# Row statistics a step later, the second head's mask at a step's end, and weight pieces last in one step of a top-k attention and MLP kernel

## The chip, the cores and the metric

The kernel runs on one core of one Trainium2 chip. The metric is device time in microseconds (us). The kernel before takes 1806.68 us, the median of three runs that lie between 1806.41 and 1808.73. The profiled execution took 1802.7 us, and its span from first to last instruction is 1800.9 us; all times within the kernel below count from the start of that span. A difference of 0.2% (3.6 us) is about the smallest that can be told from no change.

## What is computed

The reference, cut to what matters (8 batches, 8 heads, 576 rows, head size 64, model width 512):

```python
scores = scale * np.matmul(q, k.transpose(0, 1, 3, 2))
kth = np.partition(scores, -32, axis=-1)[..., -32:-31]
scores = np.where(scores >= kth, scores, -1000000000.0)
attn = np.exp(scores - max); attn = attn / (attn.sum(-1) + 1e-9)
x = (attn @ v)                      # heads side by side: (8, 576, 512)
mu, var = mean(x), mean((x - mu) ** 2)
xn = (x - mu) / np.sqrt(var + 1e-06) * g_ln
out = x + np.maximum(xn @ w_ch1, 0.0) @ w_ch2    # 512 -> 2048 -> 512
```

q, k and v are float32. The two weight matrices arrive as float64 (a float32 array times a float64 scalar) and are turned into float32 inside the kernel. Everything on the matrix engine is float32.

## The kernel before

**Units and steps.** A unit is one tile of 128 query rows (or the last 64 rows, a "rest" unit) of one batch for a pair of heads, one "tile" t = 0, 1 per head. There are 160 units. The order of everything is written out by hand: the loop `for n in range(END)` emits one step after another, and each engine runs its own instructions in just the order in which they were emitted. Buffers and semaphores only make an engine wait; nothing is reordered by a scheduler.

**What a step holds.** Step n works on several units at once:

- `scores(n+1)` (L318 to L337): the score products of the next unit on PE into four short PSUM buffers, and four copies to SBUF on ACT.
- `select(n, 0..3)` (L354, L359): four rounds of "the eight largest" and "replace them" on DVE, which find the 32nd largest score. This is DVE's main work, about 9.6 us for a whole unit and about 5.3 to 5.6 us for a rest unit.
- `prepare(n-1)` (L371, L372): the exponent's bias from the largest and the 32nd largest score, two small operations on POOL.
- `mask(n-1, t)` (L375) on ACT, and `weigh(.., t)` (L384), the exponential on ACT with its row sum. For the first eight units (`EARLY`) mask and weigh follow each other in one step; later, weigh is in the step after the mask.
- `turn` (L408 to L438): transposes of the exponentials on PE (`tp`) and their copies to `pt` on ACT: part 0, part 1 and the last part.
- `values(g)` (L461, L468, L473) for a finished group of units: the product with v on PE (`av`), copied to `oT` on ACT.
- `place(g)` (L477, L500): transposes of `oT` on PE (`xo`), and the division by the sum on ACT, which writes the rows `x`. `place_rest` (L507) does this for the rows `r` of two batches' rest units.
- When a tile of rows has its last head pair, `arrived` calls `Block.stats` (L526 to L528): mean and variance on DVE and the subtraction of the mean ("centring") on POOL, in place. In the kernel before this is the last thing but a `fill` in the step that placed the rows, after `select(n, 3)`.

PSUM has five short buffers (`psps`), shared in turn by scores, `av`, `tp` and `xo`, and three for the MLP's sums.

**The MLP.** `Block.items` makes a list of MLP pieces for two or three tiles of rows: `turn` (L552, L557, the transposes of the rows), `hidden` (L565, first product, with a relu on ACT at L577 after each fourth) and `project` (L582, second product, finished on ACT at L591 and POOL at L595). `give(n)` puts a block on the list `todo` at a fixed step. `fill()`, called eight times in a step, takes pieces from the front of the list, in order, as long as an allowance `owed` lasts. The allowance grows by `share` per call, which is an eighth of the difference between the planned DVE time of the step and the planned PE time of its attention work. In some steps the planned PE time is the larger (steps that make a value product while a rest unit is in selection): the allowance grows by nothing there. What is left on the list at the end is emitted after the last step.

**Weight pieces.** 32 pieces of the weights are converted in steps -1 to 15, two at a time: `fetch`, then `split` (three ACT operations at L175 to L179 and a clamp on POOL at L180), a step later `shift` on DVE (L183) and `join` on POOL (L189, L193, L194). `weights(n, 0)` and `weights(n, 1)` stand before and in the middle of a step.

**The first rows' step.** Step 8 is special: the last unit of the first batch's first group (`quick`) is turned, multiplied with v and placed in one step, so that the first MLP block can start in step 9.

Of the kernel before, what the change touches and what calls it, by code (L numbers as in the profile page):

```python
# [9 lines left out]
AF = mybir.ActivationFunctionType  # L10
# [18 lines left out]
def kernel(  # L29
# [39 lines left out]
    nc = tc.nc  # L69
# [8 lines left out]
    scale = 1.0 / float(D) ** 0.5  # L78
# [131 lines left out]
    batches = {}  # L210
# [22 lines left out]
    todo = []  # L233
    share = [0.0]
    owed = [0.0]
# [7 lines left out]
        owed[0] -= cost  # L243
        run()

    def fill():
        owed[0] = min(owed[0] + share[0], 6.0)
        while todo and owed[0] >= todo[0][1] / 2 and (not todo[0][3] or todo[0][3]()):
            pop()


# [8 lines left out]
    def load(job, first, second):  # L260

        job.ins = {}
        for name, src, queue in (("k", k, first), ("q", q, second)):
            t = ldpool.tile([P, S], FP32, tag=name + "in", name=name + "in")
            for i in range(P // 32):
                head, d0 = 2 * job.hp + i * 32 // D, i * 32 % D
                queue.dma_start(
                    t[i * 32 : (i + 1) * 32, :].rearrange("b (n a) -> b n a", a=32),
                    src[job.b, head, :, d0 : d0 + 32].rearrange("(n b) a -> b n a", b=32),
                )  # L270
            job.ins[name] = t
# [93 lines left out]
    def prepare(u):  # L365

        nt = len(u.tiles)
        u.bias = small.tile([P, 2], FP32, tag="bias", name="bias")
        u.e = epool.tile([P, 2, S], FP32, tag="e", name="e")
        b = u.bias[:, 0:nt]  # L370
        nc.gpsimd.tensor_tensor(b, u.thr[:, 0:nt, 7], u.top[:, 0:nt, 0], ALU.subtract)  # L371
        nc.gpsimd.tensor_scalar_mul(b, b, scale)  # L372

    def mask(u, t):
        nc.scalar.activation(  # L375
            u.e[:, t], u.sc[:, t], AF.Prelu, bias=u.thr[:, t, 7:8], scale=-1.0, alpha=SLOPE
        )
# [64 lines left out]
    xs, xps, rs, oTr, dr = {}, {}, {}, {}, {}  # L442
# [69 lines left out]
    class Block:  # L512
        def __init__(self, tiles, dsts):
            self.n = len(tiles)
            self.tiles, self.dsts = tiles, dsts
            self.x = {}
            self.mv = None
            self.ready = False

        def stats(self, i):  # L520
            x = self.x[i]
            if self.mv is None:
                self.mv = small.tile([P, J, 2], FP32, tag="mv", name="mv")
                self.rstd = small.tile([P, J], FP32, tag="rstd", name="rstd")
            st = small.tile([P, 6], FP32, tag="st", name="st")
            nc.vector.bn_stats(out=st[:], in_=x)  # L526
            nc.vector.bn_aggr(out=self.mv[:, i, :], in_=st[:])
            nc.gpsimd.tensor_scalar_sub(x, x, self.mv[:, i, 0:1])  # L528

        def std(self):  # L530
            nc.scalar.activation(
# [8 lines left out]
        def items(self):  # L540
            n = self.n
            N = n * P
            xT = [None]
            hT = {}
            ps = {}

            def turn_x(i):
                if i == 0:
                    xT[0] = xtpool.tile([P, NC, 3 * P], FP32, tag="xT", name="xT")
                tp = turned()  # L550
                for c in range(NC):
                    nc.tensor.transpose(  # L552
                        tp[:, c * P : (c + 1) * P],
                        self.x[i][:, c * P : (c + 1) * P],
                        ident[:],
                    )
                nc.scalar.copy(  # L557
                    xT[0][:, :, i * P : (i + 1) * P],
                    tp[:].rearrange("p (c j) -> p c j", j=P),
                )  # L560

            def hidden(f, c):
                if c == 0:
                    ps["h"] = product("hps")
                nc.tensor.matmul(  # L565
                    ps["h"][:, 0:N],
                    w1[:, c, f * P : (f + 1) * P],
                    xT[0][:, c, 0:N],
                    start=(c == 0),
                    stop=(c == NC - 1),  # L570
                )
                if c == NC - 1:
                    per = J // n if n in (1, 2) else 1
                    if f % per == 0:
                        hT["h"] = hpool.tile([P, J * P], FP32, tag="h", name="h")
                    hT[f] = hT["h"][:, f % per * N : (f % per + 1) * N]
                    nc.scalar.activation(hT[f], ps["h"][:, 0:N], AF.Relu)  # L577

            def project(i, f):
                if f == 0:  # L580
                    ps["o"] = product("ops")
                nc.tensor.matmul(  # L582
                    ps["o"][:],
                    hT[f][:, i * P : (i + 1) * P],
                    w2[:, f, :],
                    start=(f == 0),
                    stop=(f == NF - 1),
                )
                if f == NF - 1:
                    o = opool.tile([P, DM], FP32, tag="o", name="o")  # L590
                    nc.scalar.activation(  # L591
                        o[:], ps["o"][:], AF.Identity,
                        bias=self.mv[:, i, 0:1], scale=self.rstd[:, i : i + 1],
                    )
                    nc.gpsimd.tensor_tensor(o[:], o[:], self.x[i], ALU.add)  # L595
                    for dst, rows in self.dsts[i]:
                        nc.sync.dma_start(dst, o[rows, :])

            per_row = 1.71e-3
            return (  # L600
                [("turn", 0.44, lambda i=i: turn_x(i), None) for i in range(n)],
                [
                    (
                        "hidden",
                        max(per_row * N, 0.31),
                        lambda f=f, c=c: hidden(f, c),
                        lambda f=f, c=c: done(ready[f * P // DM * NC + c]),
                    )
                    for f in range(NF)
                    for c in range(NC)  # L610
                ],
                [
                    (
                        "project",
                        per_row * DM,
                        lambda i=i, f=f: project(i, f),
                        lambda f=f: done(ready[NF + f]) and (f < NF - 1 or self.ready),
                    )
                    for i in range(n)
                    for f in range(NF)  # L620
                ],
            )
# [13 lines left out]
    units = []  # L636
# [11 lines left out]
    for j in jobs:  # L648
        j.twin = next((x for x in fresh if (x.b, x.hp) == (j.b, j.hp)), None)
        if j.twin is None:  # L650
            fresh.append(j)


    EARLY = jobs[NHP].first


# [77 lines left out]

        return max(0.0, dve_cost(n) - pe_cost(n)) / SLOTS

    recips = {}

    def arrived(key, x):
        blk, i = block_of[key]  # L740
        blk.x[i] = x
        blk.stats(i)

    load(fresh[0], nc.sync, nc.scalar)

    nc.scalar.copy(gcol[:, 0:1], eps[:])
# [9 lines left out]
    for n in range(END):  # L756
# [9 lines left out]
        parts = turn(ex) if ex else []  # L766
        early = ex is not None and n - 1 < EARLY
        last = ex and ex is ex.group.units[-1]

        if ex and not early:  # L770
            weigh(ex, 0)
# [5 lines left out]
            select(u, 0)  # L777
        for den in recips.pop(n, []):
            nc.vector.reciprocal(den, den)
        if mk:  # L780
            prepare(mk)
        if early:
            for t in range(2):
                mask(ex, t)
                weigh(ex, t)
        weights(n, 0)
        fill()
        if ex and len(ex.tiles) > 1 and not early:
            weigh(ex, 1)
# [7 lines left out]
        if n in turns:  # L797
            turn_heads(turns[n])
            later = fresh.index(turns[n]) + 1
            if later < len(fresh):  # L800
                load(fresh[later], nc.sync, nc.sync)
        for blk in gives.get(n - 1, []):
            blk.std()
        weights(n, 1)
        fill()
        if mk and not early:
            mask(mk, 0)
# [1 line left out]
            place(g)  # L809
        if late:  # L810
            place_rest(late.job.b, late.job.hp)
        fill()
        if mk and len(mk.tiles) > 1 and not early:
            mask(mk, 1)
        fill()
        if len(parts) > 2:
            parts[1]()
# [11 lines left out]
        fill()  # L829
        if parts:  # L830
            parts[-1]()
        fill()
        for x in (u if n < EARLY else None, mk if n > EARLY else None):
            if x and x is units[x.job.last]:
                load_values(x.job)
        quick = ex.group if last and ex.group.quick else None
        if quick:

            values(quick)
            for den in recips.pop(n + 1):  # L840
                nc.vector.reciprocal(den, den)
            place(quick)
        if u:
            select(u, 3)
        for x in (g, quick):
            if x and x.job.hp == NHP - 1:
                for qt in x.qts:
                    if qt < J:
                        arrived((x.job.b, qt), xs[x.job.b, qt])
        if late and late.job.hp == NHP - 1:  # L850
            r = late.job.b // 2
            arrived(("r", r), rs[r])
        fill()
    while todo:
        pop()
# [31 lines left out]
```

## Time and profile before

| what | value |
|---|---|
| time, median of 3 | 1806.68 us |
| span of the profiled run | 1800.9 us |
| PE matmuls | 1682.3 us busy, 7401 records |
| PE weight loads | 1011.0 us busy |
| DVE | 1500.0 us busy |
| ACT | 1145.3 us busy |
| POOL | 292.0 us busy |
| `max8` and `match_replace` (L354, L359) | 1451.7 us on DVE, about 745 ns each |
| `project` matmuls (L582) | 1152 records, 546.0 us |
| `hidden` matmuls (L565) | 2048 records, 551.5 us |
| all DMA | 66.69 MB, 37 GB/s over the span |

How to read it: a float32 matmul leaves two records in the trace, so 1152 records are 576 matmuls. Busy shares are averages over stages that differ much: up to 135 us there is no MLP work and PE waits; from there to 1621 us selection on DVE and MLP on PE run side by side; from 1621 us to the end there is only MLP work. A matmul's end is modelled in the trace, so the distance from one start to the next tells more of PE than its busy time does. Where a wait is for several semaphores, the one that came last is named.

### The profile page before, as it was taken

To read this page: it belongs to the slowest core of one execution; us is meant where nothing else is said; L and a number is where in the kernel's file an instruction comes from. 1 tells how busy PE (TensorE), PEld (TensorE's weight loads), DVE (VectorE), ACT (ScalarE), POOL (GpSimd) and SP (SyncE) were. 2 spreads that over 40 slices of the span, in tenths; PEclk is the share of its full clock that TensorE was granted. 3 is DMA by queue.
4 is the path that set the end of the run, shared out by engine and by line. 5 is a ranking of instruction groups with operands and counts; after the bars stand their busy time and mean duration, and the time that the engine had idled before them with its cause. 6 is when DMAs were issued, how large, how long until landed. Compare 5 with 4: busy or idle time off the path is not lost.

```text
span 1800.9 us, 23419 instructions
## 1 busy us (share of the span) xinstructions
PE 1682.3 (93%) x7401; PEld 1011.0 (56%) x7401; DVE 1500.0 (83%) x3144; ACT 1145.3 (64%) x2846; POOL 292.0 (16%) x545
## 2 busy tenths in 40 slices
PE   3669989999799999999999999999999999999998
PEld 2337456564454574655546665565545746575565
DVE  7869899999888999989998999899998999870000
ACT  6768876675565776667757776687667766682111
POOL 4665510100100111010111010111001010101000
PEclk9659999999899999999999999999999999999999
DMA  7423231002110112002110121101201210000000
GB/s 176 108 78 90 55 66 35 25 7 46 26 28 20 33 27 48 18 20 46 31 34 20 26 46 27 31 16 43 42 13 25 41 33 20 20 20 12 0 18 12
DMA packets 249348, 66.69 MB, mean 37 GB/s; under 512 B 240517, under 2 KB 240521, under 8 KB 249225
## 3 DMA queue, kind: packets, MB, share of 16 engines
q1 hardware_dynamic: 244488, 64.61, 16.1%
q10 hardware_dynamic: 4736, 0.59, 0.3%
q8 instruction: 59, 0.97, 0.2%
q14 instruction: 65, 0.52, 0.1%
HBM read 55.71 MB, written 9.44 MB: 36 GB/s over the span
## 4 chain that ended last, share of the span: by engine, by line
PE 54%; DVE 20%; issue 11%; ACT 9%; POOL 5%; DMA 0%; POOLq 0%; DVEq 0%; SPq 0%; ACTq 0%
PE ops L582 19%; PE hps L565 17%; DVE m L354 10%; DVE wk L359 8%; PE scps L337 7%; PE av L461 5%; PE tp L408 4%; ACT e L375 2%; ACT pt L420 2%; PE av L468 2%; ACT e L384 1%; ACT x L477 1%; POOL w L194 1%; POOL size L189 1%; POOL size L193 1%
## 5 line engine op out<-in xcount | busy, mean ns | idle before, releaser
L354 DVE MAX8 m<-wk 128x8 f32<-128x576 f32 x864 | 612.8, 746 | 2.0
L565 PE MATMUL hps<-xT,w 128*128 128x256 f32 (+1 forms) x2048 | 551.5, 414 | 2.0 <-ACT xT L557 1.4
L582 PE MATMUL ops<-w,h 128*128 128x512 f32 x1152 | 546.0, 604 | 0.0
L565 PEld LDWEIGHTS hps<-xT,w 128*128 128x128 f32 x2048 | 377.0, 193 | 111.2 <-issue 22.6
L359 DVE MATCH_REPLACE8 wk<-m,wk 128x576 f32<-128x576 f32 x576 | 423.7, 742 | 0.0
L582 PEld LDWEIGHTS ops<-w,h 128*128 128x128 f32 x1152 | 203.9, 193 | 185.9 <-issue 182.2
L337 PE MATMUL scps<-kT,qT 64*128 64x288 f32 (+3 forms) x1344 | 265.2, 442 | 45.2 <-ACT pt L420 17.3
L318 ACT COPY sc<-scps 128x288 f32<-128x288 f32 x576 | 198.7, 416 | 89.7 <-PE scps L337 82.1
L337 PEld LDWEIGHTS scps<-kT,qT 64*128 64x128 f32 (+1 forms) x1344 | 138.2, 181 | 179.2 <-issue 46.4
L384 ACT ACTIVATE e<-e,bias 128x576 f32<-128x576 f32 x288 | 227.8, 791 | 14.5 <-POOL bias L372 13.3
L354 DVE MAX8 m<-sc 128x8 f32<-128x576 f32 x288 | 203.3, 743 | 40.2 <-ACT sc L318 39.8
L408 PE MATMUL tp<-ident,e 128*128 128x128 f32 x1152 | 184.1, 285 | 49.4 <-ACT e L384 49.2
L408 PEld LDWEIGHTS tp<-ident,e 128*128 128x128 f32 x1152 | 145.8, 146 | 143.6 <-ACT e L384 69.5
L375 ACT ACTIVATE e<-sc,m 128x576 f32<-128x576 f32 x288 | 220.4, 779 | 0.9 <-DVE m L354 0.9
L359 DVE MATCH_REPLACE8 wk<-m,sc 128x576 f32<-128x576 f32 x288 | 211.9, 742 | 0.0
L420 ACT COPY pt<-tp 128x512 f32<-128x512 f32 x256 | 150.3, 587 | 78.5 <-PE tp L408 77.0
L577 ACT ACTIVATE h<-hps 128x256 f32<-128x256 f32 (+1 forms) x256 | 105.8, 413 | 145.4 <-PE hps L565 144.1
L461 PE MATMUL av<-pt,vb 128*64 128x256 f32 (+2 forms) x1088 | 148.7, 415 | 3.9 <-ACT pt L420 2.3
L371 POOL TENSOR_TENSOR bias<-m,m 128x2 f32<-128x2 f32 (+1 forms) x160 | 31.1, 194 | 688.1 <-DVE m L354 639.2
L461 PEld LDWEIGHTS av<-pt,vb 128*64 128x64 f32 x1088 | 73.6, 143 | 71.7 <-issue 24.8
L473 ACT COPY oT<-av 128x256 f32<-128x256 f32 (+2 forms) x68 | 26.2, 386 | 112.8 <-PE av L468 112.7
L595 POOL TENSOR_TENSOR o<-o,x 128x512 f32<-128x512 f32 x32 | 40.7, 1271 | 350.3 <-ACT o L591 345.4
(65 smaller groups left out, 1017.8 us busy)
## 6 DMA issues: line engine op xcount, KB each, us to landing
vb<-in_v_dram SPq DMA_DIRECT2D x136, 128.0 KB, 2.5
raw<-in_moe_w_ch_dram SPq DMA_DIRECT2D x32, 512.0 KB, 4.3
kin<-in_k_dram SPq DMA_DIRECT2D x128, 72.0 KB, 2.5
qin<-in_q_dram SPq DMA_DIRECT2D x120, 72.0 KB, 2.6
out_dram<-o SPq DMA_DIRECT2D x32, 256.0 KB, 2.1
ends<-in_v_dram SPq DMA_DIRECT2D x136, 16.0 KB, 2.2
dr<-den SPq DMA_DIRECT2D x64, 0.2 KB, 1.8
out_dram<-o SPq DMA_DIRECT2D x8, 128.0 KB, 2.4
```

The lines of the kernel that those rows point to most:

```text
L318: nc.scalar.copy(u.sc[:, t, s * HALF : (s + 1) * HALF], made[s][t][:, 0:HALF])
L337: nc.tensor.matmul(ps[i * R : i * R + ql, o : o + width], qT[r, q0 : q0 + ql], kT[r, k0 : k0 + width], start=True, stop=True,)
L354: nc.vector.max(m[:, t, :], u.cur[t])
L359: nc.vector.match_replace(u.wk[t][:], m[:, t, :], u.cur[t], LOWEST)
L375: nc.scalar.activation(u.e[:, t], u.sc[:, t], AF.Prelu, bias=u.thr[:, t, 7:8], scale=-1.0, alpha=SLOPE)
L384: nc.scalar.activation(u.e[:, t], u.e[:, t], AF.Exp, bias=u.bias[:, t : t + 1], scale=-scale / SLOPE, accum_out=g.den[:, col : col + 1],)
L408: nc.tensor.transpose(ps[:, c * P : (c + 1) * P], u.e[:, t, c * P + t * R : (c + 1) * P + t * R], ident[:],)
L420: nc.scalar.copy(g.pt[:, t * J : (t + 1) * J, q0 : q0 + P], ps[:].rearrange("p (c n) -> p c n", n=P),)
L461: nc.tensor.matmul(av[h * D : (h + 1) * D, 0 : g.nq], vb[:, h * J + c, :], g.pt[:, h * J + c, 0 : g.nq], start=(c == 0), stop=False,)
L565: nc.tensor.matmul(ps["h"][:, 0:N], w1[:, c, f * P : (f + 1) * P], xT[0][:, c, 0:N], start=(c == 0), stop=(c == NC - 1),)
L577: nc.scalar.activation(hT[f], ps["h"][:, 0:N], AF.Relu)
L582: nc.tensor.matmul(ps["o"][:], hT[f][:, i * P : (i + 1) * P], w2[:, f, :], start=(f == 0), stop=(f == NF - 1),)
```

## The change

The change has five parts.

1. `prepare` of the first 16 units (`CONVERTING` is 14 + 2) goes from POOL to ACT: a multiplication by the scale and one small activation per tile, three ACT operations instead of two on POOL. In these steps POOL is also converting weights.
2. Rows' statistics and centring wait for the following step: `arrived` only notes the rows for step n+1, and `blk.stats` runs there after `select(n, 1)`; for the very first rows (step 9, `gives_first`), already after `select(n, 0)`. A row tile's `turn` piece may be taken from the list only once its centring has been emitted (`centred`).
3. The mask of the second tile, `mask(mk, 1)`, goes from the middle of a step, ahead of the turns of parts 1 and last, to behind them.
4. The `fill` after `place` takes at least one piece, whatever the allowance, in steps that place rows.
5. In the first rows' step (`quick`, step 8), both halves of the weight pieces' work come after the rows have been placed.

The purpose is to take waits for ACT off DVE's queue, to take waits for POOL off ACT's, and to let copies out of PSUM come sooner.

```diff
-    def fill():
+    def fill(least=0):
         owed[0] = min(owed[0] + share[0], 6.0)
-        while todo and owed[0] >= todo[0][1] / 2 and (not todo[0][3] or todo[0][3]()):
+        while todo and (not todo[0][3] or todo[0][3]()):
+            if owed[0] < todo[0][1] / 2 and least <= 0:
+                break
+            least -= 1
             pop()
...
         b = u.bias[:, 0:nt]
+        if u.i < CONVERTING:
+
+            nc.scalar.mul(b, u.thr[:, 0:nt, 7], scale)
+            for t in range(nt):
+                nc.scalar.activation(
+                    b[:, t : t + 1], u.top[:, t, 0:1], AF.Identity,
+                    bias=b[:, t : t + 1], scale=-scale,
+                )
+            return
         nc.gpsimd.tensor_tensor(b, u.thr[:, 0:nt, 7], u.top[:, 0:nt, 0], ALU.subtract)
...
             nc.gpsimd.tensor_scalar_sub(x, x, self.mv[:, i, 0:1])
+            self.centred.add(i)
...
-                [("turn", 0.44, lambda i=i: turn_x(i), None) for i in range(n)],
+                [("turn", 0.44, lambda i=i: turn_x(i), lambda i=i: i in self.centred) for i in range(n)],
...
-    def arrived(key, x):
+    def arrived(n, key, x):
         blk, i = block_of[key]
         blk.x[i] = x
-        blk.stats(i)
-
+        rows_of.setdefault(n + 1, []).append((blk, i))
...
+        if n == gives_first:
+            for blk, i in rows_of.pop(n):
+                blk.stats(i)
...
-        weights(n, 0)
+        if not quick:
+            weights(n, 0)
         fill()
...
+        for blk, i in rows_of.pop(n, []):
+            blk.stats(i)
         for blk in gives.get(n - 1, []):
             blk.std()
-        weights(n, 1)
+        if not quick:
+            weights(n, 1)
...
-        fill()
-        if mk and len(mk.tiles) > 1 and not early:
-            mask(mk, 1)
+        fill(1 if g or late else 0)
         fill()
...
         if parts:
             parts[-1]()
+        if mk and len(mk.tiles) > 1 and not early:
+            mask(mk, 1)
         fill()
...
             place(quick)
+            weights(n, 0)
+            weights(n, 1)
```

More of the change, by code (lines that the diff above doesn't have):

```diff
@@ L517, in __init__ @@
             self.mv = None
+            self.centred = set()
             self.ready = False
@@ L651 @@
             fresh.append(j)
+    for i, u in enumerate(units):
+        u.i = i
+    CONVERTING = max(n for n in batches if batches[n]) + 2
     EARLY = jobs[NHP].first
@@ L735, in slot @@
         return max(0.0, dve_cost(n) - pe_cost(n)) / SLOTS
-    recips = {}
-    def arrived(key, x):
+    recips, rows_of = {}, {}
+    def arrived(n, key, x):
         blk, i = block_of[key]
         blk.x[i] = x
-        blk.stats(i)
+        rows_of.setdefault(n + 1, []).append((blk, i))
+    gives_first = min(gives)
     load(fresh[0], nc.sync, nc.scalar)
@@ L768 @@
         last = ex and ex is ex.group.units[-1]
+        quick = ex.group if last and ex.group.quick else None
         if ex and not early:
@@ L835 @@
                 load_values(x.job)
-        quick = ex.group if last and ex.group.quick else None
         if quick:
@@ L848 @@
                     if qt < J:
-                        arrived((x.job.b, qt), xs[x.job.b, qt])
+                        arrived(n, (x.job.b, qt), xs[x.job.b, qt])
         if late and late.job.hp == NHP - 1:
             r = late.job.b // 2
-            arrived(("r", r), rs[r])
+            arrived(n, ("r", r), rs[r])
         fill()
```

## The prediction

> **What bounds the kernel now.** I read the page first (busy shares and slices), then waits by engine, then sums by window, then the timeline of two stretches.
>
> ```profile
> PE 1682.3 (93%) x7401; PEld 1011.0 (56%) x7401; DVE 1500.0 (83%) x3144; ACT 1145.3 (64%) x2846; POOL 292.0 (16%) x545
> ...
> DVE  7869899999888999989998999899998999870000
> ```
>
> DVE stops in slice 36 of 40; about 180 us of pure MLP follow, the same 26 projects, two transposed blocks and their products in both builds, so the tail costs the same. Before there is any MLP work, from 45 to 90 and from 90 to 135 us, the windows view gives a granted PE clock of 0.65 and 0.56.
>
> DVE's waits, columns total, times, longest:
>
> ```profile
> DVE st L526 <- ACT x L477: 54.3, 13, 8.8
> DVE m L354 <- ACT sc L318: 39.8, 16, 4.8
> DVE size L183 <- POOL size L180: 12.4, 8, 2.9
> DVE den L779 <- ACT den L396: 9.6, 1, 9.6
> ...
> ACT e L384 <- POOL bias L372: 13.3, 5, 4.1
> ```
>
> The change takes the first row away almost whole. Whether that is time depends on the second: where DVE also waits for scores (m L354 <- sc), PE and ACT are the late ones, and a DVE that comes earlier only waits there longer. So look at PE in one period of 20 steps (windows view; PE, weight load, DVE, ACT, POOL busy):
>
> ```profile
> 768.00:962.00 194.00, 190.43 (x812) 102.39 (x812) 186.05 (x391) 132.42 (x326) 21.81 (x53) 0.99 0.15 31
> ```
>
> PE leaves 3.6 of 194 us, DVE 8. By distances from start to start (429 ns per 128x512 record when packed, 215 per 128x256, 322 per 128x384, 109 per transpose) PE is packed in nearly every step. The exceptions return: steps that place rows while a rest unit is selected, where the allowance gives no MLP piece (timeline, first PE, then ACT: start, length, engine, line, operation, out<-in, and in brackets the idle time before it and what ended it).
>
> ```profile
> 858.84 0.44 PE L500 MATMUL xo<-ident,oT 128*128 128x128 f32 x2
> 859.60 0.66 PE L408 MATMUL tp<-ident,e 128*128 128x128 f32 x4 [0.33 <-ACT e L384]
> 860.10 0.27 PE L437 MATMUL tp<-ident,e 128*128 128x128 f32 x1
> 860.30 2.02 PE L337 MATMUL scps<-kT,qT 64*128 64x288 f32 x6
> 862.70 0.75 PE L337 MATMUL scps<-kT,qT 64*128 64x288 f32 x2 [0.39 <-ACT pt L420]
> 863.38 1.25 PE L565 MATMUL hps<-xT,w 128*128 128x384 f32 x2
> ```
>
> ```profile
> 861.38 0.80 ACT L375 ACTIVATE e<-sc,m 128x576 f32<-128x576 f32 x1
> 862.04 0.61 ACT L420 COPY pt<-tp 128x512 f32<-128x512 f32 x1
> ```
>
> PE stands 0.49 us between xo and tp (859.11 to 859.60), and its scores take 3.1 us (860.30 to 863.38) where an unhindered set takes 1.17 (854.63 to 855.80): the fourth of the five short buffers comes free only with the copy at 862.04, which stands on ACT behind the second mask at 861.38. That is 2.4 us per such step, and there are 28 (30, 33, 36, 39, 42, 45, 48, 51, then four in each period).
>
> The start is another matter: POOL, ACT and PE hold one another up.
>
> ```profile
> 91.53 0.20 POOL L371 TENSOR_TENSOR bias<-m,m 128x2 f32<-128x2 f32 x1
> 91.60 0.43 DVE L183 TENSOR_SCALAR size<-size 128x512 uint32<-128x512 uint32 x1 [2.85 <-POOL size L180]
> ...
> 131.71 0.69 DVE L526 BATCH_NORM_STATS2 st<-x 128x6 f32<-128x512 f32 x1 [8.79 <-ACT x L477]
> ...
> 134.41 0.66 PE L552 MATMUL tp<-ident,x 128*128 128x128 f32 x4 [1.93 <-POOL x L528]
> ```
>
> **What the Trainium skill says.** "Perfetto Trace Analysis", Identifying the Most-Contended Engine: a PE's busy share is no measure of how full it is. The trace agrees: 93% busy, yet 4 of 20 steps hide 2.4 us. "TensorE: Matmul & The Clock Gate", Architectural detail (the array is 16x): ACT, DVE and GpSimd queues are strictly first in, first out. It agrees: the bias at 91.53 needed a result that DVE had at 82.0, and stood behind two weight pieces. Same page, What's actually happening: the clock is halved until activity lifts it; the 0.56 to 0.65 at the start agrees. Price: "ScalarE: Activation LUTs", What ACT_TABLE_LOAD costs: 186 ns plus 0.833 ns per element, about 93 ns more with a pointer bias, 93 ns overlapped.
>
> **Part by part.**
>
> Bias on ACT (16 units). The trace has no such operation; nearest is ACT den L396, 128x4 at 205 ns. By the page 0.19 + 2 x 0.28 - 2 x 0.09 = 0.56 us (estimate); if each waits for the one before, 0.9. I take 0.6. Against it stand the 13.3 us of waits for POOL's bias in the first eight units. Net by den of step 8 (before: 121.2): 13.3 - 8 x 0.6 = 8.5; about 1 goes where unit 1 is held by DVE instead; 7.6 us earlier. In steps 9 to 16 the bias only costs ACT; 1 us for that.
>
> Weight pieces last in step 8. Between den and the last copy to pt ACT loses six split operations at 0.57, of which 2.75 us reach the value product (its first record at 123.62, the bulk at 125.75, against pt copies that now follow each other). So x is ready 7.6 + 2.75 = 10.4 us earlier, near 121.6. But POOL now has split and join ahead of the centring: ACT size 0.7, clamp 0.6, joins 2 x (1.28 + 1.27) = 5.1, second clamp 0.6 bring it to 128.6; centring 1.6; first row transpose at 130.3 against 134.4. Gain 4.1 us. DVE reaches step 9 some 15 us earlier, but PE does not need it.
>
> Statistics in the next step. DVE's own 0.86 us per tile only move. Behind them stand selection rounds, which are then waited for by masks a step later; DVE is not late there. The 54.3 us of DVE waits are therefore worth nothing by themselves, save 1.2 at step 18 (the stage to 266 us is held by DVE: PE waits 3.39 us for qT at 265.66). A price comes where PE takes the rows at once. Step 31: PE is ready near 346; DVE starts the step at 344.1 (345.8 less two moved statistics), the statistics now come after select 1, 5.5 us into it, at 349.6, and the tiles are centred at 352.1 and 353.6. PE is back at the same piece 2.5 us later than before, step 30's gain already used up. Step 44: the r rows were taken at 471.91 after a wait of 6.39. Now 470.03 - 3.06 - 0.86 (wait and r statistics gone) + 5.62 + 0.86 + 1.67 = 474.26, less a tp part put ahead, 0.6: 1.75 us lost. Step 19 waits too, inside PE's spare time. All later blocks sit behind other pieces by steps: nothing.
>
> Mask at the end and a forced piece. The pt copy starts where the mask did, at 861.38 instead of 862.04: 0.66 us. The forced piece fills the gap and the wait for buffers, so its length (0.86, 0.64 or 0.43 us) vanishes from the packed step that follows; the instruction order of the build shows it taken from there. Step 42 has nothing to take; step 30 is used above. Of the other 26: 13 projects, 6 of 384, 7 of 256 columns: 11.2 + 3.8 + 3.0 = 18.0, plus 26 x 0.66 = 17.2: 35.2 us. The mask in its new place lies in ACT's waits for PE (0.8 us before the last copy and the relu). Step 16's forced piece: 1 us.
>
> End: the tp wait of 1.90 at 1619.6 shrinks, 1.5.
>
> Sum: 4.1 - 1 + 1.2 + 1 - 2.5 - 1.75 + 35.2 + 1.5 = 37.75. 1806.7 - 37.7 = 1769.
>
> Does DVE have room? Without waits it needs 186.6 us in the period 768 to 962; PE then needs 193.7 - (0.64 + 3 x 0.86 + 4 x 0.66) = 187.8. Just.
>
> **Rivals.**
>
> A: PE stays as packed as it is, and the new gaps fill only with waits (DVE or ACT comes last in those steps). Only the start and the turns count: 4.1 + 1.2 - 4.25, about 1, to 8 with half the terms: 1799 to 1806. For it: DVE's room of 1 us per period. Against: the waits named are ACT's, and DVE loses 5 us of waits per period.
>
> B: DVE is the bound and its waits come out whole: 54.3 + 12.4 = 67, 1740. For it: DVE at 83% and 94% in the middle. Against: PE's packing.
>
> C: slower. Centring lies behind the joins without x coming earlier (the ACT and PE round at the start not loosened): +4; steps 31 and 44 lose 5 and 4; no piece hidden: 1806.7 + 13 = 1820. For it: PE is in order, and a turn it cannot make stops everything. Against: only four blocks are taken at once.
>
> **How the numbers follow.** Forecast 0.74, A 0.12, B 0.09, C 0.05. Around the forecast: 0.66 and the piece's length could each be half true (17 us less gain), the start is worth 0 to 8, and better filled steps could spare PE clock dips (up to 8 more). That gives 1750 to 1788 with some of B's way; I give 1750 to 1790. Faster by over 0.2% needs under 1803: forecast, B and a half of A.
>
> **What would show it.** DVE st waits near zero, waits for sc larger than 39.8. First row transpose near 130. In the placing steps pt copies right after the x copies, and the last score pair 0.66 us sooner. PE waits for POOL's x near 6 us at step 31. If PE waits for e or DVE grow in the middle, A is right; if the start moves by much more than 4 us, my POOL queue is wrong.

## The result, and the profile after

| | before | after |
|---|---|---|
| median | 1806.55 us (4 runs, 1806.13 to 1808.73) | 1762.1 us (4 runs, 1760.61 to 1763.47) |
| ratio, 95% interval | | 0.9751, 0.9735 to 0.9768 |
| span of the profiled run | 1800.9 us | 1758.8 us |

The changed kernel is 44.5 us faster (2.5%); 1769 was forecast, with a range of 1750 to 1790. The profiled runs differ by 42.1 us. The forecast holds, but the sum behind it has a term missing and several that are too good, and the part of the change that its title names first, the later statistics, turns out to cost time.

The page of the changed kernel, the engines' busy time and the slices of DVE:

```profile
PE 1650.1 (94%) x7401; PEld 1003.4 (57%) x7401; DVE 1499.0 (85%) x3144; ACT 1153.3 (66%) x2894; POOL 285.6 (16%) x513
...
DVE  7988899989989999999999999999999999950000
```

DVE does the same work (1499.0 against 1500.0 us) in a shorter time. PE is busy 32 us less with the same 7401 records: the ends of matmuls are modelled, and time at half clock counts as busy.

DVE's waits of the changed kernel (total, times, longest):

```profile
DVE m L357 <- ACT sc L321: 35.5, 15, 8.2
...
DVE st L539 <- ACT x L489: 9.0, 2, 7.2
```

The wait for placed rows (`st`) is nearly gone, 54.3 to 9.0 us, but the wait for scores (`m <- sc`) did not grow in its place: 39.8 to 35.5. The sum of the two fell by 49.6 us, about as much as the kernel got shorter. Why that is no proof that DVE's waits were the cost is shown by the third experiment.

The period that the prediction looked at (20 steps; windows view: us, then PE, weight load, DVE, ACT and POOL busy, granted PE clock, DMA share, GB/s) now lies here in the changed kernel:

```profile
748.10:935.20 187.10, 186.72 (x820) 102.84 (x819) 185.56 (x390) 132.68 (x329) 21.76 (x53) 1.00 0.16 32
```

PE leaves 0.4 us of 187.1 (3.6 of 194 before), DVE 1.5 (8 before). The prediction put PE's need at 187.8 us and DVE's at 186.6, and said that DVE just has room. That is what came.

The placing step shown before at 858.84 now reads so on PE (timeline: start, length, engine, line, operation, out<-in, count):

```profile
841.74 0.44 PE L512 MATMUL xo<-ident,oT 128*128 128x128 f32 x2
842.01 0.81 PE L579 MATMUL hps<-xT,w 128*128 128x384 f32 x2
842.66 0.60 PE L420 MATMUL tp<-ident,e 128*128 128x128 f32 x4
843.10 0.27 PE L449 MATMUL tp<-ident,e 128*128 128x128 f32 x1
843.30 2.77 PE L340 MATMUL scps<-kT,qT 64*128 64x288 f32 x8
```

and so on ACT:

```profile
844.28 0.52 ACT L591 ACTIVATE h<-hps 128x384 f32<-128x384 f32 x1
844.65 0.62 ACT L432 COPY pt<-tp 128x512 f32<-128x512 f32 x1
845.11 0.32 ACT L450 COPY pt<-tp 128x128 f32<-128x128 f32 x1
845.27 0.84 ACT L387 ACTIVATE e<-sc,m 128x576 f32<-128x576 f32 x1
```

Between `xo` and `tp` stands the forced piece (842.01), where PE had been idle for 0.49 us, and the copy to `pt` (844.65) no longer has a mask ahead of it; the mask comes at 845.27, behind both copies. From start to start, the score products now take 2.70 us (843.30 to 846.00), which is 1.53 us more than a packed set; before it was 1.91 us. Of the 2.4 us that this step lost, 1.53 are left. It is one of the worst of its kind, since the relu of the piece (844.28) stands ahead of the copy to `pt`; in 9 of the 22 such steps after 474 us the scores lose 0.93 us only, in 9 more 1.15 to 1.25.

Two places that got worse. The turn of the rows placed in step 30, and that of the `r` rows, on PE (in brackets the idle time before and what ended it):

```profile
347.92 1.12 PE L566 MATMUL tp<-ident,x 128*128 128x128 f32 x4 [5.42 <-POOL x L541]
...
472.06 1.12 PE L566 MATMUL tp<-ident,r 128*128 128x128 f32 x4 [8.59 <-POOL r L541]
```

In the kernel before they read:

```profile
346.88 1.11 PE L552 MATMUL tp<-ident,x 128*128 128x128 f32 x4 [0.51 <-POOL x L528]
...
471.91 1.11 PE L552 MATMUL tp<-ident,r 128*128 128x128 f32 x4 [6.39 <-POOL r L528]
```

On DVE of the changed kernel, the statistics of the first stand behind two rounds of step 31's selection:

```profile
339.68 1.40 DVE L357 MAX8 m<-sc 128x8 f32<-128x576 f32 x2
...
345.22 0.69 DVE L539 BATCH_NORM_STATS2 st<-x 128x6 f32<-128x512 f32 x1
```

### The profile page after: what moved, and what is told of

The parts are those of the page before. It is cut to its first block, busy times and chain, and to the rows that moved or that the text cites. A ratio compares the mean times of both kernels' runs of the same rounds, so it can differ in the third digit from the quotient of the medians.

```text
span 1758.8 us, 23377 instructions
## 1 busy us (share of the span) xinstructions
PE 1650.1 (94%) x7401; PEld 1003.4 (57%) x7401; DVE 1499.0 (85%) x3144; ACT 1153.3 (66%) x2894; POOL 285.6 (16%) x513
## 4 chain that ended last, share of the span: by engine, by line
PE 63%; issue 10%; DVE 8%; ACT 4%; POOL 1%; POOLq 0%; DVEq 0%; ACTq 0%
PE hps L579 21%; PE ops L596 19%; PE scps L340 9%; PE av L473 6%; PE tp L420 5%; DVE m L357 4%; DVE wk L362 3%; PE av L480 2%; ACT e L387 1%; PE tp L566 1%; PE xo L512 1%; ACT oT L485 1%; PE tp L449 1%; ACT pt L432 1%; ACT x L489 0%
## 5 line engine op out<-in xcount | busy, mean ns | idle before, releaser
L340 PE MATMUL scps<-kT,qT 64*128 64x288 f32 (+3 forms) x1344 | 252.2, 441 | 33.5 <-DVE qT L296 20.1
L357 DVE MAX8 m<-sc 128x8 f32<-128x576 f32 x288 | 203.7, 744 | 36.3 <-ACT sc L321 35.5
L387 ACT ACTIVATE e<-sc,m 128x576 f32<-128x576 f32 x288 | 225.7, 784 | 1.5 <-DVE m L357 0.8
L473 PE MATMUL av<-pt,vb 128*64 128x256 f32 (+2 forms) x1088 | 144.7, 409 | 0.5 <-ACT pt L443 0.5
```

The source lines that it names most:

```text
L340: nc.tensor.matmul(ps[i * R : i * R + ql, o : o + width], qT[r, q0 : q0 + ql], kT[r, k0 : k0 + width], start=True, stop=True,)
L357: nc.vector.max(m[:, t, :], u.cur[t])
L387: nc.scalar.activation(u.e[:, t], u.sc[:, t], AF.Prelu, bias=u.thr[:, t, 7:8], scale=-1.0, alpha=SLOPE)
L473: nc.tensor.matmul(av[h * D : (h + 1) * D, 0 : g.nq], vb[:, h * J + c, :], g.pt[:, h * J + c, 0 : g.nq], start=(c == 0), stop=False,)
```

## Where the time went

I compared the start of every unit's score products on PE in the two traces (those of unit n + 1 stand in step n). The changed kernel is ahead of the kernel before by:

| up to | lead, us | what lies between |
|---|---|---|
| unit 31 | 4.1 | the start and step 16's piece |
| unit 34 | -0.4 | step 30's piece, and the turn of its rows, which waits: -4.5 |
| unit 45 | 4.4 | placing steps: +4.8 |
| unit 46 | 2.2 | turn of the `r` rows: -2.2 |
| unit 159 | 43.8 | 23 placing steps, and the clock: +41.6 |
| end | 42.1 | -1.7 |

The clock is the missing term. In the trace's record of the granted PE clock, the kernel before has six stretches at half clock between 474 and 1700 us, 27.3 us in all; the changed kernel has none. At half clock, half of that time is lost: 13.7 us. The steps bear this out: in five of them whose forced piece is a project piece the lead grows by 1.82 or 1.83 us up to the next score products, and in two more, where the kernel before had a stretch of 3.4 us behind the same place, by 3.52 and 3.53. What remains of the 41.6 us is 27.9. One placing step, near 490 us, is longer than the others in every kernel and has 0.3 of it; 22 like ones have about 1.25 us each.

One of these stretches, in the windows view of the kernel before, just behind the placing step of 858.84:

```profile
863.80:867.20 3.40, 3.40 (x7) 1.77 (x6) 3.40 (x8) 1.94 (x7) 2.48 (x4) 0.50 0.00 0
```

and the same place in the changed kernel:

```profile
846.70:850.10 3.40, 3.40 (x15) 2.11 (x14) 3.33 (x8) 3.37 (x12) 1.66 (x2) 1.00 0.43 68
```

In the first PE calls itself busy for all of the 3.40 us, at a clock of 0.50, with 7 records; in the second it does 15.

Stretches before 474 us are not counted here. Most of them lie at the start and at the two turns, where PE waits long. One matters below: at the turn of step 30's rows the kernel before has 6.8 us at half clock and the changed kernel 10.2.

## The experiments

The times of one table; "half clock" is the number and the total length of the stretches that begin between 474 and 1700 us in the profiled run.

| kernel | median, us | ratio to before, 95% interval | half clock |
|---|---|---|---|
| before (profiled run) | 1806.55 | | 6, 27.3 us |
| after | 1762.1 | 0.9751 (0.9735 to 0.9768) | 0 |
| e1 after, statistics at once | 1754.79 | 0.9709 (0.9688 to 0.973) | 1, 3.4 us |
| e2 before + piece + mask | 1754.64 | 0.971 (0.9692 to 0.9727) | 1, 3.4 us |
| e3 before + statistics later | 1821.73 | 1.0074 (1.0045 to 1.0102) | 12, 58.0 us |
| e4 after without the piece | 1781.62 | 0.986 (0.9842 to 0.9879) | 1, 6.8 us |
| e5 after without the mask's move | 1793.74 | 0.9921 (0.9904 to 0.9938) | 7, 30.7 us |
| e6 after, bias on POOL | 1766.48 | 0.9776 (0.9761 to 0.979) | 2, 6.8 us |
| e7 after, pieces as before | 1759.35 | 0.9733 (0.9718 to 0.9747) | 0 |
| e8 e1, centring ahead of the pieces | 1750.99 | 0.9689 (0.9674 to 0.9703) | 1, 6.8 us |
| e9 before + mask | 1771.37 | 0.9795 (0.9781 to 0.981) | 1, 3.4 us |
| e10 before + piece | 1787.21 | 0.9875 (0.9859 to 0.9892) | 7, 27.3 us |
| e11 before + start | 1812.56 | 1.0017 (1.0005 to 1.0029) | 7, 34.1 us |

The kernel before ran again beside each group: 1808.77 us beside e1 to e4, 1806.28 beside e5 to e8, 1807.68 beside e9 to e11. e5 to e8 ran on another chip than the rest of e1 to e11.

### Which part brings the gain: e1 to e4

The theory P is that of the prediction: PE is the bound, and its holes in the placing steps are the cost. D is the rival that DVE's waits for placed rows were the cost.

e1 puts the statistics back to the end of the placing step:

```diff
 def arrived(n, key, x):
     blk, i = block_of[key]
     blk.x[i] = x
-    rows_of.setdefault(n + 1, []).append((blk, i))
+    blk.stats(i)
```

> The kernel after, with only the statistics and the centring put back to the end of the step that placed the rows (the gate on the turn is then always open). Theory P (PE and its buffers are the bound, DVE comes second by about 1 us in a period of 20 steps): DVE gets its wait of some 5 us per period back, needs about 192 us in a period where the eased PE needs 187, so 4 to 5 us per period come back over five to six periods; the delays at steps 31 and 44 (4.9 and about 2 us in the trace of after) vanish. Together 1775 to 1790. Theory D (DVE's waits for the placed rows were the cost all along): nearly the whole gain is lost, 1798 to 1808.

Measured: 1754.79 us. Both theories missed, and the changed kernel gets faster without its moved statistics: the intervals of the ratios do not touch, and 0.9709 against 0.9751 is 7.6 us (5.6 between the profiled spans). DVE's waits of e1:

```profile
DVE st L539 <- ACT x L489: 26.8, 13, 8.4
DVE m L357 <- ACT sc L321: 20.1, 6, 5.6
```

My expectation for P was wrong in one point. I counted some 5 us in each period for a wait of DVE that comes back. It does come back, 26.8 us of it, but it is no cost of a fixed size: DVE stands ahead of PE and waits just as long as it is ahead, and a shorter wait for scores makes up for it (20.1 instead of 35.5). e1 is ahead of the changed kernel from one place on: at unit 32's score products its lead over the kernel before is 0.1 us, at unit 33's it is 3.7, where the changed kernel falls from 3.8 to -0.4. The same turn on PE in e1:

```profile
345.72 0.66 PE L566 MATMUL tp<-ident,x 128*128 128x128 f32 x4 [1.04 <-POOL x L541]
```

It waits 1.04 us instead of 5.42. So 4.4 of the 7.7 us that the two kernels differ by here are the wait. The clock has about 3 more, by estimate: the half-clock stretch of the changed kernel lasts from 343.9 to 354.1 us, 6.2 us beyond the end of the wait at 347.92, and e1 has none here. From unit 46 on the two kernels keep a distance of 3.4 to 6.3 us.

e2 goes the other way, the kernel before with only the forced piece and the mask's move (`fill(1 if g or late else 0)` and `mask(mk, 1)` behind the last turn, as in the change's diff):

> The kernel before, with only the forced piece after placing and the second mask at the step's end. P: the placing steps are eased (about 33 us, and some 10 us of PE clock dips), but DVE's waits remain and hold it back by 4 to 5 us a period: 1780 to 1793. D: the waits for placed rows stay, so at most 3 us: 1803 to 1807.

Measured: 1754.64 us, the same as e1. The two edits bring the whole gain and 7 us more; all else in the change costs that. The expectation of P was 25 us and more too slow, by the same mistake as in e1: without DVE's 4 to 5 us a period it had 43 us of gain, and 48.4 lie between the profiled spans.

e3 moves the statistics alone, with the condition on the `turn` piece:

```diff
-        blk.stats(i)
+        rows_of.setdefault(n + 1, []).append((blk, i))
...
+        for blk, i in rows_of.pop(n, []):
+            blk.stats(i)
         for blk in gives.get(n - 1, []):
             blk.std()
```

> The kernel before, with only the statistics in the following step (with the gate on the turn). P: PE is as packed as before, DVE only waits for scores in place of rows, and PE waits longer for centred rows at steps 31 and 44: 1805 to 1814. D: 1760 to 1770.

Measured: 1821.73 us, slower than both expected. D, by which DVE's waits were the cost, falls. DVE's waits of e3:

```profile
DVE m L354 <- ACT sc L318: 84.9, 38, 8.1
...
DVE st L527 <- ACT x L477: 15.3, 4, 8.8
```

The wait for rows went from 54.3 to 15.3 us and the wait for scores from 39.8 to 84.9: together 94.1 before and 100.2 now. The edit changes the name of DVE's wait, not its amount, because PE decides when DVE may go on. The trace also tells where the 21.3 us between the profiled spans went (1800.9 to 1822.2). The turn of step 30's rows waits 5.18 us on PE, and the lead is -5.1 us at unit 33's score products. The other loss is the clock: 58.0 us at half clock instead of 27.3, so 15.4 us more lost. That moved statistics bring such stretches is not shown: e11 below has 34.1 us without them, and e9 and e10 show how much of it is chance.

e4 is the changed kernel with `fill()` where the change has `fill(1 if g or late else 0)`:

> The kernel after, without the forced piece (the fill after placing keeps to its allowance). P: each of some 26 placing steps loses the length of its piece, 18 us in all, and a few PE clock dips come back: 1778 to 1788. D: the statistics are still moved, so 1762 to 1766.

Measured: 1781.62 us, as P has it. The forced piece is worth 19.5 us in the changed kernel, of which up to 3.4 are the one half-clock stretch of this kernel; 18.0 were predicted.

### The mask, and the clock: e5, e9, e10

e5 is the changed kernel with the second mask in the middle of the step:

```diff
         fill(1 if g or late else 0)
+        if mk and len(mk.tiles) > 1 and not early:
+            mask(mk, 1)
         fill()
...
         if parts:
             parts[-1]()
-        if mk and len(mk.tiles) > 1 and not early:
-            mask(mk, 1)
```

> The changed kernel with the second head's mask back in the middle of a step, behind the forced piece of MLP; the rest stays. If the mask behind the last turn is worth the gap that it closes ahead of the last score matmuls (the chain of before shows 0.66 us in each of the 26 placing steps, 17.2 us), and the forced piece is worth its own gap, this kernel gives 1779 to 1788 us. If the forced piece alone already keeps TensorE busy (the mask only decides where the one wait of a step lies), it stays within 6 us of the changed kernel, 1760 to 1768.

Measured: 1793.74 us, above both ranges. The mask's move is worth 31.6 us, not 17.2. From start to start on PE, the score products of the same placing step lose 2.20 us (859.34 to 862.71, less 1.17 packed) against 1.53 in the changed kernel, 0.67 us: the 0.66 of the prediction. Over the 22 placing steps after 474 us it is 40.3 against 25.4 us, 0.68 a step. Its timeline on PE:

```profile
858.06 0.81 PE L579 MATMUL hps<-xT,w 128*128 128x384 f32 x2
...
859.34 1.92 PE L340 MATMUL scps<-kT,qT 64*128 64x288 f32 x6
862.03 0.75 PE L340 MATMUL scps<-kT,qT 64*128 64x288 f32 x2 [0.77 <-ACT pt L432]
```

The forced piece is there (858.06), but the last pair of scores waits at 862.03 for the copy to `pt`, as before the change. Then the clock (windows view of e5):

```profile
863.00:866.40 3.40, 3.40 (x9) 2.07 (x9) 3.33 (x9) 2.15 (x8) 2.58 (x2) 0.50 0.61 99
```

Seven such stretches, 30.7 us, cost 15.4 us that the changed kernel does not pay. 17.2 + 15.4 = 32.6, against 31.6 measured.

This gave a new pair of theories. In all kernels here, each half-clock stretch after 474 us starts 3 to 6 us behind the `xo` transposes of a step that places rows, but for one of e3 at 481 us. (There are 60 such steps in 1226 us, and 3 us behind each make up only a seventh of the time.) The question is whether the stretches come with any hole, or need a long one. Two kernels with one edit each tell it. e9 is the kernel before with this alone:

```diff
-        if mk and len(mk.tiles) > 1 and not early:
-            mask(mk, 1)
         fill()
...
         if parts:
             parts[-1]()
+        if mk and len(mk.tiles) > 1 and not early:
+            mask(mk, 1)
```

> The kernel before with the second head's mask behind the last turn and nothing else: no forced piece, statistics at once, start as before. Two theories on the half-clock stretches of TensorE. G, gaps only: each of the 26 placing steps loses its 0.66 us, 17.2 in all, and the six half-clock stretches after 474 us (27.3 us in the kernel before, 13.7 us of work lost) stay: 1787 to 1791 us. W, the longest single gap decides: the gap ahead of the last score pair is down to 1.24 us, as in the kernel without the forced piece, which has one such stretch; nearly all go, and it takes 1776 to 1781 us with at most two of them.

e10 is the kernel before with `fill(1 if g or late else 0)` alone:

> The kernel before with the forced piece of MLP in the placing steps and nothing else; the mask stays in the middle. The pieces are worth 18 us of gaps (prediction). W: the gap ahead of the last score pair stays at 1.60 us, as in the changed kernel with the mask in the middle, so five or more half-clock stretches stay: 1785 to 1792 us. If any fuller step is enough to keep the clock: at most two stretches and 1775 to 1779 us.

Measured: 1771.37 and 1787.21 us, with one half-clock stretch (3.4 us) and seven (27.3 us). W, by which a long hole is needed, is right in the count of both and in the time of e10; e9 is 5 us faster than W's range and further from that of G, by which any hole will do. The placing step of e9 that was shown above for the others, on PE:

```profile
845.09 0.44 PE L500 MATMUL xo<-ident,oT 128*128 128x128 f32 x2
845.85 0.66 PE L408 MATMUL tp<-ident,e 128*128 128x128 f32 x4 [0.33 <-ACT e L384]
...
846.55 2.49 PE L337 MATMUL scps<-kT,qT 64*128 64x288 f32 x8
848.98 1.24 PE L565 MATMUL hps<-xT,w 128*128 128x384 f32 x3
```

It loses 0.49 us ahead of `tp` and 1.26 within its score products (2.43 from start to start, less 1.17), 1.75 in all. The steps of e10 lose nothing ahead of `tp` and 1.60 to 2.28 within the scores.

The loss within the score products sorts the 22 like placing steps of all thirteen profiles, 286 steps. 195 of them lose 1.61 us or less, and none of these is followed by a stretch. 91 lose 1.8 us or more, and 30 of these are (in nine the stretch begins ahead of the last score products and makes the loss longer). So W had its limit too low: the ten steps of e10 with 1.60 us, which it counted on, brought no stretch, and five of the twelve with 1.8 to 2.3 did. Which of the long ones are hit is a matter of timing. In each trace, all changes of the granted clock lie on one grid of 3.41 us. In 19 of the 91 long steps a point of that grid falls 3.1 to 3.56 us behind the first score product, and a stretch begins at all 19; the other 11 begin somewhat earlier or later (2.3 to 4.1 us). In 38 of the 195 shorter steps a point falls there as well, and none begins, so it isn't luck that spared these.

The table says the same of all kernels. With the mask at the end (score products lose 0.93 to 1.25 us in 18 of the 22 steps of the changed kernel) there are at most two stretches, and most of these lie near 490 us, at the one placing step that is longer in every kernel (2.7 to 4.1 us in its scores). With the mask in the middle (1.59 us and more, 1.91 in the kernel before) there are six to twelve. Not separated is what exactly has to be long: the longest single gap, the loss within the score products or the loss of the whole step (e9's 1.75 us lies below 1.8 too).

The mask's move is thus worth more than the forced piece, though the prediction had them at 17.2 and 18.0: alone it takes 36.3 us off (1807.68 to 1771.37), of which 17.2 are the holes and 12 the clock of the profiled run ((27.3 - 3.4) / 2). Of the other 7 us, some 5 are a matter of which run was profiled: between the profiled spans lie 31.4 us (1800.9 to 1769.5), and the runs of the kernel before reach from 1802.75 to 1813.34 us. About 2 us stay open.

### The start: e6, e7, e8, e11

e6 leaves the bias on POOL (`if u.i < 0:`), e7 has the weight pieces of step 8 at their usual places (`weights(n, 0)` and `weights(n, 1)` without `if not quick`):

> The changed kernel with the bias of the first units on GpSimd again, the rest as changed. By the theory that the start's gain is lost again in the stage that VectorE holds (steps 11 to 22), the total moves by less than 4 us: 1760 to 1766, although the first turn of rows comes later. If the bias on ScalarE is what brings the start's lead of 4 us to the end, it takes 1766 to 1770.

> The changed kernel with the weight pieces of the first rows' step at their usual places in the step, not last. The centring then no longer waits behind the joins of these pieces on GpSimd, but the first rows are placed behind them. By the theory that only the order up to the first turn changes and VectorE's stage swallows it: 1758 to 1765. If pieces last is what the start's gain rests on: 1766 to 1769.

Measured: 1766.48 and 1759.35 us. The bias on ACT is worth 4.4 us in the changed kernel, at the border of what the two theories gave; in the traces e6 is behind by 4.5 us at unit 31 already. Pieces last seems to cost something: 2.8 us by the medians and 1.4 between the profiled spans, less than can be told from no change by the times alone, since the intervals of the two ratios overlap. The reason is in POOL's timeline of the changed kernel:

```profile
119.45 1.28 POOL L189 TENSOR_TENSOR size<-size,low 128x512 uint32<-128x512 uint32 x1
120.80 1.28 POOL L194 TENSOR_TENSOR w<-size,sign 128x512 f32<-128x512 f32 x1
122.04 1.25 POOL L189 TENSOR_TENSOR size<-size,low 128x512 uint32<-128x512 uint32 x1
123.38 1.34 POOL L194 TENSOR_TENSOR w<-size,sign 128x512 f32<-128x512 f32 x1
124.69 0.61 POOL L180 TENSOR_SCALAR size<-size 128x512 f32<-128x512 f32 x1
125.28 3.37 POOL L541 TENSOR_SCALAR x<-x,mv 128x512 f32<-128x512 f32 x2
```

The centring (L541) waits behind two joins and a clamp, as the prediction said, and PE waits for it:

```profile
127.16 1.12 PE L566 MATMUL tp<-ident,x 128*128 128x128 f32 x4 [8.53 <-POOL x L541]
```

With the pieces at their usual places this turn stands at 125.42, with a wait of 1.92 us.

e8 is e1 with the order that follows from this: in step 8, statistics and centring come ahead of the pieces, and the bias is on ACT for one unit less.

```diff
             place(quick)
-            weights(n, 0)
-            weights(n, 1)
...
             arrived(n, ("r", r), rs[r])
+        if quick:
+            weights(n, 0)
+            weights(n, 1)
         fill()
```

> The kernel with the statistics at the end of the placing step (measured at 1754.8 us with the rest as changed), and in the first rows' step statistics and centring ahead of that step's weight pieces, and the bias on ScalarE one unit less. If the joins of the pieces on GpSimd hold the first turn and the lead stays: 1748 to 1753. If VectorE's stage behind it (steps 11 to 22) swallows whatever the start gains: 1754 to 1756.

Measured: 1750.99 us, 3.8 us faster than e1, and the fastest of all: 3.1% off the kernel before. In its timeline the centring on POOL comes first,

```profile
121.06 3.31 POOL L541 TENSOR_SCALAR x<-x,mv 128x512 f32<-128x512 f32 x2 [9.97 <-ACT size L175]
124.34 0.61 POOL L180 TENSOR_SCALAR size<-size 128x512 f32<-128x512 f32 x1
```

and the first turn is at 122.88 us, 5.6 earlier than in e1 (128.46). Of this, 1.7 us are left at the last score products in the traces. The other 1.7 us between the profiled spans (1753.2 to 1749.8) are the half-clock stretch of e1, which lies at 1570 us, behind its last score products; the intervals of the two ratios overlap.

e11 is the kernel before with the start's two edits alone:

> The kernel before with the two edits of the start alone: bias on ScalarE in the first units and the pieces last in the first rows' step; statistics at once, mask in the middle, no forced piece. If VectorE's stage up to step 22 swallows what the start gains, as the equal times of the two kernels with and without the start's edits said: 1804 to 1809 us. If the start's 4 us of the prediction reach the end: 1800 to 1803 us. Half-clock stretches that come or go by chance move it by 1.7 us each.

Measured: 1812.56 us, 12 runs from 1805.24 to 1813.57. With the statistics at once, the start as it stands in the change brings nothing, as e1 against e2 had said: its first turn comes 5.6 us earlier than before (128.81), and by unit 19 the lead is 0.5 us. The median lies beyond the expected range. The mean clock of these 12 runs goes with their time (0.961 of the whole span at 1805.24 us, 0.955 at 1813.57), so the median probably tells mostly how many of the long holes met a loss of the clock.

## Why the prediction was right, point by point

- **PE is the bound, and its holes in the placing steps are the cost: right.** Filled holes bring 4.8 + 27.9 = 32.7 us in the trace; 35.2 were predicted. Per step, from start to start on PE, the sizes are the predicted ones: with a project piece 1.51 us (0.86 + 0.66), with 384 columns 1.30 (0.64 + 0.66), with 256 columns 1.10 (0.43 + 0.66). Four steps bring only 0.8 to 0.9: in two of them a relu of the MLP comes ahead of the copy to `pt` on ACT, as at 844.28 above, in the other two (scores at 682.61 and 1030.89 us) the last ACT operation of a finished output tile, and it delays what the mask no longer delays. I had counted these as free.
- **The clock: the missing term.** I named it ("better filled steps could spare PE clock dips (up to 8 more)") but left it out of the sum. It is 13.7 us in the profiled runs, and the runs e4, e5, e9 and e10 show that the mask's move brings it, not the piece. The page "TensorE: Matmul & The Clock Gate" of the Trainium skill could have told me more: its section What's actually happening gives a free-running window of about 3.4 us, and this trace agrees: the stretches behind 474 us are one or two such lengths (3.4 or 6.8 us) and lie on a grid of 3.41 us. But its rule against gaps, in Why this matters for your kernels, speaks of gaps of about 3 us between bursts, and here losses of 1.8 to 2.3 us within a set of score products were enough. Its section A second HAM failure mode: psum-queue depth-cycling, on short idle times behind PSUM buffers, is nearer to this case.
- **That the 54.3 us of DVE's waits are worth nothing by themselves: right.** In e3 most of them are gone (15.3 left), and the kernel is 13 us slower, in part by the clock; in e1 half of them are back, and it is 7 us faster than the changed kernel.
- **The turn of step 30's rows: mis-sized.** 2.5 us were predicted, 4.5 came. The delay itself is as predicted, 5.2 us (352.1 against 346.88 in the prediction; in the trace 347.92 against 346.88 less the lead of 4.1). The step that failed is that PE would be only 2.5 us later behind it, as if half had been made up; it made up 0.7 us. The half-clock stretch at this place (10.2 us against 6.8) was not in the sum either.
- **The `r` turn:** 1.75 predicted, 2.2 measured.
- **The start: the mechanism right, the sizes by chance.** The order on POOL is the predicted one, but the first turn came at 127.16 instead of 130.3, 7.3 us earlier than before and not 4.1: POOL reached the first clamp at 118.87, and the sum had that at 122.3. From unit 25 to unit 31 the lead is 4.1 us, where the terms gave 5.3. It depends on the later statistics: without them the start's edits bring nothing (e11, e1 against e2), and one of the two may cost something (e7). The bias took 0.23 + 0.48 us on ACT for a unit (82.24 and 82.50 in its timeline); 0.6 was taken, near the estimate of 0.56 from the prices on the page "ScalarE: Activation LUTs", What ACT_TABLE_LOAD costs. The two activations overlap by 0.09 us, as that page has it, but neither overlaps with the multiplication that they read.
- **The end: wrong sign.** 1.5 us were to be gained, 1.7 were lost. The wait at `tp` did not shrink, it grew from 1.90 to 2.24 us (at 1576.49). Most of the rest is order and no loss at the end: behind unit 159's score products the changed kernel has 706 PE records and the kernel before 700, and the six are pieces of the hidden product of 0.215 us each, so 1.3 us of the lead there are work put off.
- **What would show it.** `st` near zero: 9.0. PE's wait for POOL's `x` near 6 us at step 31: 5.4. A start that moves by much more than 4 us was to speak against the POOL queue; the first turn moved by 7.3, with POOL in the predicted order. `m <- sc` above 39.8: wrong, 35.5, since the quicker PE shortens that wait too. Copies to `pt` directly behind those to `x`: yes, but for the relu.

The sum of the prediction was 37.75 us; with the measured sizes it is 4.1 - 4.5 + 4.8 - 2.2 + 27.9 + 13.7 - 1.7 = 42.1. That the total came out so near is luck: the clock made up for the turns, the end and the shorter gains. Rival A (new gaps fill with waits only) fell with 0.4 us left on PE in a period; rival B named the wrong engine; rival C had the right reasons for a loss in its turns, and e3 is such a kernel.

## What to carry to other kernels

A wait of an engine that runs ahead is no cost, whatever its total: look for the holes of the engine that is behind, and fill them with its own work or free its buffers sooner. Where TensorE loses close to two microseconds in one place of otherwise packed work, look at the granted clock behind it, since the hole may cost a half-clock stretch as well; here it was enough to bring the loss down to 1.6 us, without closing it. An edit that moves work "off the queue" to a later step must be checked at the few places where another engine takes that work at once; here two such places cost more than the move brought at the start.

## What was not expected of the hardware

Half-clock stretches of 3.4 or 6.8 us follow a loss of 1.8 to 2.3 us in PE's packing within some 3 us (30 of 91 steps), and no step with a loss of 1.61 us or less was followed by one (195 steps, 13 profiles). Each takes up to half its length, 1.7 or 3.4 us. Which of 22 like steps is hit changes from kernel to kernel, with the place where the 3.41 us grid of the clock falls. It probably changes from run to run as well, since the times spread where there are such steps: e11's 12 runs, with the same instructions, over 8.3 us, the 4 runs of the changed kernel over 2.9 and those of e9 over 0.4.
